# Layer norm's 1/sqrt as a power on GpSimd, first loads in halves, and a new order of the first block in a fused norm, Mish and filter kernel

## The chip, the core and the metric

One core of a Trainium2 chip runs the whole program. It has five engines, each with its own instruction stream: TensorE (PE in the profile) multiplies matrices, VectorE (DVE) and ScalarE (ACT) compute on tiles, GpSimd (POOL) does so too, and SyncE (SP) here only issues transfers. ACT can issue transfers as well. The engines meet only where one waits for what another has produced. The metric is the time of one execution on the device in microseconds; each comparison takes the median of several.

## What is computed

The input x has 2,048 rows (time) of 640 columns. Each row is normalized, and the output is x plus two branches of the normalized rows: a filter along time with a kernel built from the parameters, and a dense layer to 1,728 columns, Mish, and a dense layer back to 640.

```
xn  = (x - mean(x)) / sqrt(var(x) + 1e-5)            # per row
A   = causal_conv(xn, K) + xn * D_skip               # K from log_A, A_imag, C, dt: 128 modes
h   = xn @ w1 + b1                                    # 640 -> 1728
B   = (h * tanh(softplus(h))) @ w2                    # Mish, 1728 -> 640
out = x + A + B
```

For the parameters given here the modes hardly decay or turn, so the filter is computed as two running sums along time. The kernel tests on the chip whether the values allow this and its number formats, and holds a general path for other values, which does not run here.

## The kernel before, in words

**Numbers.** Products of float32 precision are made from float16 matmuls: every operand is split into a high part, rounded to float16, and a low part, the float16 of what is left. A product takes three matmuls: high by high, low by high, high by low. ScalarE makes the high parts (`hi_w1`, L371; `hi_w2`; `hi0`, L844), VectorE the low parts (`lo_w1`, L375; `lo_w2`, L382; `lo0`, L847).

**Tiling.** The rows are four blocks `b` of 512 (four tiles of 128 rows), the 1,728 columns are 14 groups `f`, of 128 columns but for one of 64 (f = 8), and the 640 columns are five chunks `k` of 128. Step (b, f) (`step`, L761) multiplies block b with group f of w1 into one PSUM bank (`mm1`, L545), passes it through Mish on ScalarE and VectorE (`mish_...`, L607 to L657), and three steps later multiplies the result with group f of w2 into five accumulators (`mm2`, L566). Block 0's steps also load w1 and w2 and split them. Next to this, each step has side work in lists that `place` (L676) fills: `LOADS` are transfers, `A_` and `E_` go to ScalarE, `V_` and `W_` to VectorE, earlier and later in the step. Side work is: the statistics of the next block's four tiles (steps 2 to 5), their 1/sqrt (`rstd` at step 5, L755, with `rstd_ops`, L401: thirteen small VectorE operations, a bit trick and three Newton steps, and a copy), a transpose and a round trip through DRAM that spread mean and 1/sqrt over the partitions (`spread`, L415, step 7), normalizing and splitting the next block (steps 8 to 13; `norm_t`, `hi_x` at L385, `lo_x`), the parameters of the filter (`mode_ops`, L439, cut into pieces by the list at L693), the filter itself in blocks 1 to 3, and the tests.

**The order** is written out by hand: each engine runs its instructions in the order of the program, and waits where an operand is not there yet. A tile's buffer is taken again when its last reader is done; the eight buffers of the weights (tag `w`) are such a ring.

**Block 0's beginning** is code of its own (L810 to L933). Tiles 0 and 1 fill the first 256 columns of the transposed block (slice `CA`), tiles 2 and 3 the other 256 (`CB`). The four tiles of x are loaded; VectorE computes mean and variance (`stat_ops`, L395: two halves, then an aggregation). The root is computed by both engines: ScalarE takes a square root (`sqrt0`, L814) and VectorE refines it and takes reciprocals (`rstd0`, L818), for tiles 0 and 1 together, then for 2 and 3 one by one. Tiles 0 and 2 are normalized on VectorE (`norm0`, L828), 1 and 3 on ScalarE (`norm0_a`, L831). TensorE, which has run 15 filler products (`fill`, L850), transposes a tile in five pieces (`to_t0`, L840), ScalarE takes the high parts (`hi0`) and VectorE the low parts (`lo0`), and TensorE multiplies with the first three groups of w1 piece by piece (`mm1_part`, L538, L543): first for CA, then for CB. In the order of each engine, the statistics of tile 2 precede the low part of w1(0) on VectorE, and those of tile 3 follow it. The first transfers stand at L856 to L870:

```
for i in range(2):
    sp.dma_start(X0[:, i, 0:320], xr[0, i, :, 0:320])
    a.dma_start(X0[:, i, 320:D], xr[0, i, :, 320:D])
load_w1(0)
a.dma_start(X0[:, 2], xr[0, 2])
sp.dma_start(X0[:, 3], xr[0, 3])
load_w1(1, a)
a.activation(warm, one, AF.Sqrt)
```

The last of these lines loads ScalarE's table for the square root; another one loads that of the sigmoid at L902.

## Time and profile before

| | us |
|---|---|
| median of 3 runs | 374.67 (374.29, 374.67 and 1362.29) |
| the profiled execution, its own time | 374.67 |
| its span, first to last instruction | 372.9 |
| TensorE busy | 361.2 |
| VectorE busy | 322.2 |
| ScalarE busy | 272.7 |
| GpSimd busy | 0.9 |

Times in the profile are us from the start of the span. A row of a timeline gives start, duration, engine, line of the kernel, operation, output and inputs by the program's names, shapes, how many instructions are merged, and in brackets how long the engine had been idle before and what ended that. "PEld" is the load of weights into TensorE, which overlaps its products. Matmuls overlap each other, so that a duration of one is more than its distance to the next. "xh", "xl", "w1h", "w1l" are high and low parts. Rows of GpSimd are rough in their spans.

### The profile page before, as it was taken

The page shows a single profiled execution, that of the slowest core. Times are in us where ns is not written, and L with a number is a line of the kernel's source. Part 1 is how long each engine was busy: PE and PEld are TensorE (multiplying, and loading weights), DVE is VectorE, ACT ScalarE, POOL GpSimd, SP SyncE. Part 2 cuts the span into 40 slices and gives each one's busy share as a digit, 9 for nine tenths or more (in the row PEclk, how much of TensorE's full clock was granted, in tenths as well). Part 3 has the DMA queues.
Part 4 walks back from the last instruction along what each step waited for, and adds up shares of the span by engine and source line. Part 5 has one row for each costly group of instructions (what it writes and reads, how often), then busy time and mean ns, then how long its engine had stood idle before and what let it go on. Part 6 is the DMA issues. An engine that isn't in the chain of part 4 may idle for free.

```text
span 372.9 us, 5013 instructions
## 1 busy us (share of the span) xinstructions
PE 361.2 (97%) x1737; PEld 168.8 (45%) x1737; DVE 322.2 (86%) x591; ACT 272.7 (73%) x525; POOL 0.9 (0%) x9
## 2 busy tenths in 40 slices
PE   7899999999999999999999999999999999999992
PEld 6654444444444444444444444444444444444441
DVE  4979988999997999778779999978896899999952
ACT  4799866979866858788858875598977676788540
POOL 1000000000000000000000000000000000000000
PEclk9999999999999999999999999999999999999998
DMA  7756953590002163412752252512410021300003
GB/s 261 261 159 216 307 192 127 144 352 0 2 0 73 38 198 82 153 38 70 238 167 66 60 179 83 174 39 88 127 48 32 0 78 64 113 0 2 0 7 142
DMA packets 23039, 40.81 MB, mean 109 GB/s; under 512 B 3080, under 2 KB 6432, under 8 KB 23008
## 3 DMA queue, kind: packets, MB, share of 16 engines
q1 hardware_dynamic: 22432, 39.45, 33.0%
q10 hardware_dynamic: 576, 0.98, 0.8%
q8 instruction: 15, 0.25, 0.3%
q14 instruction: 16, 0.13, 0.1%
HBM read 35.17 MB, written 5.26 MB: 108 GB/s over the span
## 4 chain that ended last, share of the span: by engine, by line
PE 73%; DVE 14%; ACT 7%; issue 2%; DMA 2%; ACTq 0%; DVEq 0%
PE h L564 35%; PE acc L591 10%; PE acc L593 10%; PE acc L592 10%; DMA x<-in_A_u_dram 2%; DVE A L640 2%; DVE A L632 1%; DVE g L518 1%; DVE g L523 1%; DVE lo L656 1%; ACT hi L646 1%; PE h L543 1%; ACT s L616 1%; PE acc L586 1%; PE acc L575 1%
## 5 line engine op out<-in xcount | busy, mean ns | idle before, releaser
L564 PE MATMUL h<-xh,w1h 128*128 128x512 f16 x265 | 92.0, 379 | 0.4 <-ACT xh L386 0.3
L593 PE MATMUL acc<-hi,w2l 128*128 128x512 f16 x235 | 89.1, 379 | 0.0
L592 PE MATMUL acc<-lo,w2h 128*128 128x512 f16 x235 | 89.1, 379 | 0.0
L591 PE MATMUL acc<-hi,w2h 128*128 128x512 f16 x235 | 89.1, 379 | 0.0
L564 PE MATMUL h<-xh,w1l 128*128 128x512 f16 x245 | 86.3, 379 | 0.0
L564 PEld LDWEIGHTS <-w1h 128*128 128x128 f16 (+1 forms) x534 | 50.5, 98 | 63.7 <-issue 4.6
L564 PE MATMUL h<-xl,w1h 128*128 128x512 f16 (+2 forms) x269 | 63.8, 377 | 0.0
L646 ACT ACTIVATE hi<-A 128x512 f16<-128x512 f32 (+1 forms) x56 | 35.0, 624 | 36.7 <-DVE A L640 36.7
L616 ACT ACTIVATE s<-h,cv 128x512 f32<-128x512 f32 x51 | 34.6, 678 | 28.3 <-PE h L564 27.1
L620 DVE SCALAR_TENSOR_TENSOR A<-h,bs,s 128x512 f32<-128x512 f32 x51 | 38.0, 745 | 12.7 <-ACT s L616 12.5
L656 DVE SCALAR_TENSOR_TENSOR lo<-A,hi 128x512 f16<-128x512 f32 x52 | 35.7, 687 | 11.7 <-ACT hi L646 11.6
L628 ACT ACTIVATE p<-p,kc 128x512 f32<-128x512 f32 (+1 forms) x56 | 40.4, 722 | 1.7
L624 ACT ACTIVATE p<-s,kc 128x512 f32<-128x512 f32 (+1 forms) x56 | 39.8, 710 | 0.1
L636 ACT ACTIVATE s<-p,kc 128x512 f32<-128x512 f32 (+1 forms) x56 | 39.8, 710 | 0.0
L632 DVE SCALAR_TENSOR_TENSOR A<-p,A 128x512 f32<-128x512 f32 (+1 forms) x56 | 38.1, 681 | 1.5 <-ACT p L628 1.5
L640 DVE SCALAR_TENSOR_TENSOR A<-s,A 128x512 f32<-128x512 f32 (+1 forms) x56 | 38.1, 681 | 0.2
L564 PEld LDWEIGHTS <-w1l 128*128 128x128 f16 x245 | 24.0, 98 | 29.3 <-issue 0.9
L591 PEld LDWEIGHTS <-w2h 128*128 128x128 f16 x235 | 23.1, 98 | 27.6
L593 PEld LDWEIGHTS <-w2l 128*128 128x128 f16 x235 | 23.0, 98 | 27.8
L592 PEld LDWEIGHTS <-w2h 128*128 128x128 f16 x235 | 23.0, 98 | 27.3
L518 DVE TENSOR_TENSOR_SCAN g<-g,car,kc 128x512 f32<-128x512 f32 x20 | 25.6, 1278 | 0.0
L523 DVE TENSOR_TENSOR_SCAN g<-g,car,g 128x512 f32<-128x512 f32 x20 | 25.4, 1270 | 0.0
(151 smaller groups left out, 357.3 us busy)
## 6 DMA issues: line engine op xcount, KB each, us to landing
res<-in_xT_dram SPq DMA_DIRECT2D x20, 256.0 KB, 5.4
out_dram<-xt SPq DMA_DIRECT2D x19, 256.0 KB, 2.7
chk<-in_w2T_dram SPq DMA_DIRECT2D x15, 288.0 KB, 3.1
w2s<-in_B_w_dram SPq DMA_DIRECT2D x13, 320.0 KB, 3.3
chk<-in_w1T_dram SPq DMA_DIRECT2D x13, 320.0 KB, 3.7
w1s<-in_w_dram SPq DMA_DIRECT2D x12, 320.0 KB, 5.0
xrow<-in_A_u_dram SPq DMA_DIRECT2D x12, 320.0 KB, 4.0
xt<-in_xT_dram SPq DMA_DIRECT2D x15, 256.0 KB, 5.8
```

Source lines behind the costliest of these rows:

```text
L564: pe.matmul(o, w, x, start=(j == 0), stop=(j == len(order) - 1))
L591: pe.matmul(ACC[k], W2H[f][:, c[k]], hi, start=False, stop=False)
L592: pe.matmul(ACC[k], W2H[f][:, c[k]], lo, start=False, stop=False)
L593: pe.matmul(ACC[k], W2L[f][:, c[k]], hi, start=False, stop=en)
L616: a.activation(s, h, AF.Sigmoid, bias=cv[:n, f:f + 1], scale=1 / SH)
L624: a.activation(p, s, AF.Arctan, bias=one[:n], scale=-1.0)
L628: a.activation(p, p, AF.Square, bias=pi4[:n], scale=2.0)
L632: v.scalar_tensor_tensor(A, p, MR, A, op0=OP.add, op1=OP.mult)
L636: a.activation(s, p, AF.Square, bias=mb[:n])
L640: v.scalar_tensor_tensor(A, s, MC, A, op0=OP.add, op1=OP.mult)
L646: a.activation(hi[:n], A, AF.Copy, scale=MA * SA / SH)
L656: v.scalar_tensor_tensor(lo, A, MA * SA / SH, hi[:n], op0=OP.mult, op1=OP.subtract)
```

## The change

- **The root.** `rstd_ops`, `sqrt0` and `rstd0` are gone. A new `rstd(var, out)` has two GpSimd instructions: add 1e-5, then raise to the power -0.5, the exponent being a constant column that takes the place of the square root's bias. In block 0 it runs for each tile by itself, right behind its statistics; in the other blocks once per block at step 5, followed by the copy of the means, on GpSimd as well.
- **First loads.** w1(0) and tiles 2 and 3 of x are loaded in halves of 64 partitions, one half on SP's queue and one on ACT's. w1(1) is loaded on SP's queue, behind tile 3. ScalarE's first table is that of the sigmoid, and there is no second load of a table in block 0's beginning.
- **The first block.** All four tiles are normalized on VectorE. The low part of w1(0) runs ahead of the statistics of tile 2. Two low parts of x (slice CA) run between the statistics of tiles 2 and 3, the others around the normalizing of tile 3. The pieces are taken in the order k = 4, 0, 1, 2, 3 (`KS`). ScalarE's high part of w1(0) stands behind tile 0's transposes in the program, ahead of the high parts of x, as before.
- **Side work.** The low parts of w2(12) and w2(13) move from step (0, 13) to steps (1, 0) and (1, 1). Of the filter's parameter operations, 13 and 15 run in steps (0, 6) and (0, 7) in place of 11 and 11, and the six of step (0, 13) are gone from there.

```
--- before.py
+++ after.py
@@ -309,9 +309,9 @@
 
 
     kc = cst.tile([P, 8], F32, name="kc")
-    for i, c in enumerate((EPS / 4, 1.0, -math.pi / 4, MB, 0.0)):
+    for i, c in enumerate((-0.5, 1.0, -math.pi / 4, MB, 0.0)):
         v.memset(kc[:, i:i + 1], c)
-    eps4, one, pi4, mb, zero = (kc[:, i:i + 1] for i in range(5))
+    half, one, pi4, mb, zero = (kc[:, i:i + 1] for i in range(5))
     warm = kc[:, 5:6]
     ident = cst.tile([P, P], F32, name="ident")
     make_identity(nc, ident)
@@ -347,10 +347,12 @@
     W1S, W2S, XT, RES, XROW, ACT, SM, NX, CHK, SK, ML = ({} for _ in range(11))
     NCHK = NF + 3 * KD
 
-    def load_w1(f, e=sp):
+    def load_w1(f, queues=(sp,)):
         W1S[f] = row.tile([P, KD, P], F32, name="w1s", tag="w", bufs=8)
-        n = FC[f]
-        e.dma_start(W1S[f][:, :, :n], w1[D * FO[f]:D * (FO[f] + n)].rearrange("(p k f) -> p k f", p=P, k=KD))
+        n, m = FC[f], P // len(queues)
+        for j, e in enumerate(queues):
+            o = D * FO[f] + j * m * KD * n
+            e.dma_start(W1S[f][j * m:(j + 1) * m, :, :n], w1[o:o + m * KD * n].rearrange("(p k f) -> p k f", p=m, k=KD))
 
     def load_w2(f):
         W2S[f] = row.tile([P, D], F32, name="w2s", tag="w", bufs=8)
@@ -398,19 +400,10 @@
         yield lambda: v.bn_stats(st[:, 1], xt[:, 320:640])
         yield lambda: v.bn_aggr(mv[:, i], st)
 
-    def rstd_ops(mv, y):
-
-        hv = tmp.tile([P, NT], F32, name="hv")
-        t = tmp.tile([P, NT], F32, name="t_rs")
-        yi = y.bitcast(I32)
-        yield lambda: v.tensor_scalar(y, mv[:, :, 1], EPS, None, op0=OP.add)
-        yield lambda: v.tensor_scalar(hv, y, 0.5, None, op0=OP.mult)
-        yield lambda: v.tensor_scalar(yi, yi, 1, None, op0=OP.logical_shift_right)
-        yield lambda: v.tensor_scalar(yi, yi, -1, 0x5f3759df, op0=OP.mult, op1=OP.add)
-        for _ in range(3):
-            yield lambda: v.tensor_tensor(t, y, y, op=OP.mult)
-            yield lambda: v.tensor_tensor(t, t, hv, op=OP.mult)
-            yield lambda: v.scalar_tensor_tensor(y, t, 1.5, y, op0=OP.subtract, op1=OP.mult, reverse0=True)
+    def rstd(var, out):
+
+        g.tensor_scalar(out, var, EPS, None, op0=OP.add)
+        g.tensor_tensor(out, out, half.to_broadcast(list(out.shape)), op=OP.pow)
 
     def spread():
 
@@ -683,14 +676,12 @@
             A_[0, f].append(lambda f=f: hi_w2(f))
             if f + 4 < NF:
                 A_[0, f].append(lambda f=f: hi_w1(f + 4))
-            if f > 0:
-                V_[0, f].append(lambda f=f: lo_w2(f - 1))
-                if f + 3 < NF:
-                    V_[0, f].append(lambda f=f: lo_w1(f + 3))
-        W_[0, LAST].append(lambda: lo_w2(LAST))
+            if f > 0 and f + 3 < NF:
+                V_[0, f].append(lambda f=f: lo_w1(f + 3))
+            V_[(0, f + 1) if f < LAST - 1 else (1, f - LAST + 1)].append(lambda f=f: lo_w2(f))
 
         LOADS[0, 4].append(lambda: SM.update(ops=mode_ops(load_par())))
-        for at, n in (((0, 6), 11), ((0, 7), 11), ((0, 13), 6), ((1, 0), 8), ((1, 1), 99)):
+        for at, n in (((0, 6), 13), ((0, 7), 15), ((1, 0), 8), ((1, 1), 99)):
             W_[at].append(lambda n=n: [o() for _, o in zip(range(n), SM["ops"])])
 
         LOADS[1, 0].append(lambda: xt_alloc(0))
@@ -702,7 +693,7 @@
                 LOADS[b, i].append(lambda b=b, i=i: load_x(b + 1, i))
                 W_[b, i + 2].append(lambda b=b, i=i: stats(b + 1, i))
             LOADS[b, 5].append(lambda b=b: load_xt(b + 1))
-            W_[b, 5].append(rstd)
+            W_[b, 5].append(rstds)
             PEX[b, 7] = spread
             for k in range(KD):
                 W_[b, 8 + k].append(lambda b=b, k=k: norm_t(b + 1, k, NX["bc"]))
@@ -752,10 +743,9 @@
         for k in range(KD):
             sp.dma_start(XT[b][:, k], xT[k * P:(k + 1) * P, b * TB:(b + 1) * TB])
 
-    def rstd():
-        for o in rstd_ops(NX["mv"], NX["st"][:, 1]):
-            o()
-        v.tensor_copy(NX["st"][:, 0], NX["mv"][:, :, 0])
+    def rstds():
+        rstd(NX["mv"][:, :, 1], NX["st"][:, 1])
+        g.tensor_copy(NX["st"][:, 0], NX["mv"][:, :, 0])
 
 
     def step(b, f):
@@ -809,21 +799,7 @@
 
     X0 = big.tile([P, NT, D], F32, name="x0", tag="bigA")
     mv0 = tmp.tile([P, NT, 2], F32, name="mv0")
-    rs0 = tmp.tile([P, 3, NT], F32, name="rs0")
-
-    def sqrt0(i, n):
-
-        a.activation(rs0[:, 0, i:i + n], mv0[:, i:i + n, 1], AF.Sqrt, bias=eps4, scale=0.25)
-
-    def rstd0(i, n):
-
-        h, r, w = (rs0[:, j, i:i + n] for j in range(3))
-        yield lambda: v.tensor_scalar(w, mv0[:, i:i + n, 1], EPS, 0.25, op0=OP.add, op1=OP.mult)
-        yield lambda: v.reciprocal(r, h)
-        for q in range(n):
-            yield lambda q=q: v.scalar_tensor_tensor(h[:, q:q + 1], w[:, q:q + 1], r[:, q:q + 1], h[:, q:q + 1],
-                                                     op0=OP.mult, op1=OP.add)
-        yield lambda: v.reciprocal(h, h)
+    rs0 = tmp.tile([P, 2, NT], F32, name="rs0")
 
     def norm0(i):
         v.tensor_scalar(X0[:, i], X0[:, i], mv0[:, i, 0:1], rs0[:, 0, i:i + 1], op0=OP.subtract, op1=OP.mult)
@@ -832,13 +808,16 @@
         v.scalar_tensor_tensor(rs0[:, 1, i:i + 1], mv0[:, i:i + 1, 0], -1.0, rs0[:, 0, i:i + 1], op0=OP.mult, op1=OP.mult)
         a.activation(X0[:, i], X0[:, i], AF.Identity, bias=rs0[:, 1, i:i + 1], scale=rs0[:, 0, i:i + 1])
 
+
+    KS = (KD - 1, *range(KD - 1))
+
     def flat0(k, c):
 
         j = k if c == CA else k + 6 if k < KD - 1 else KD
         return ACC[j // 2][:, (CA, CB)[j % 2]]
 
     def to_t0(i):
-        for k in range(KD):
+        for k in KS:
             pe.transpose(flat0(k, (CA, CB)[i // 2])[:, i % 2 * P:(i % 2 + 1) * P], X0[:, i, k * P:(k + 1) * P], ident)
 
     def hi0(k, c):
@@ -856,11 +835,12 @@
         for i in range(2):
             sp.dma_start(X0[:, i, 0:320], xr[0, i, :, 0:320])
             a.dma_start(X0[:, i, 320:D], xr[0, i, :, 320:D])
-        load_w1(0)
-        a.dma_start(X0[:, 2], xr[0, 2])
-        sp.dma_start(X0[:, 3], xr[0, 3])
-        load_w1(1, a)
-        a.activation(warm, one, AF.Sqrt)
+        load_w1(0, (sp, a))
+        for i in range(2, NT):
+            sp.dma_start(X0[:P // 2, i], xr[0, i, :P // 2])
+            a.dma_start(X0[P // 2:, i], xr[0, i, P // 2:])
+        a.activation(warm, one, AF.Sigmoid)
+        load_w1(1)
         load_w1(2)
         sp.dma_start(cv[:, 0:24], vec)
         load_w1(3)
@@ -869,60 +849,53 @@
         load_w2(1)
         load_w1(5)
         S = [list(stat_ops(mv0, X0[:, i], i)) for i in range(NT)]
-        R = {i: list(rstd0(i, n)) for i, n in ((0, 2), (2, 1), (3, 1))}
+
+        def stats0(i):
+            for o in S[i]:
+                o()
+            rstd(mv0[:, i:i + 1, 1], rs0[:, 0, i:i + 1])
+
         fill(15)
-        for o in S[0] + S[1]:
-            o()
-        sqrt0(0, 2)
-        for o in R[0]:
-            o()
-        norm0_a(1)
-        hi_w1(0)
+        stats0(0)
+        stats0(1)
         norm0(0)
         to_t0(0)
+        hi_w1(0)
+        norm0(1)
         to_t0(1)
-        for k in range(KD):
+        for k in KS:
             hi0(k, CA)
-        for o in S[2]:
-            o()
-        sqrt0(2, 1)
         lo_w1(0)
-        mm1_part(0, ("hh", "lh"), CA, start=True)
+        stats0(2)
+        mm1_part(0, ("hh",), CA, start=True, ks=KS)
+        mm1_part(0, ("lh",), CA)
         hi_w1(1)
+        lo0(KS[0], CA)
+        lo0(KS[1], CA)
         mm1_part(1, ("hh",), CA, start=True)
         hi_w1(2)
+        stats0(3)
+        norm0(2)
         mm1_part(2, ("hh",), CA, start=True)
-        for o in S[3]:
-            o()
-        sqrt0(3, 1)
-        for o in R[2]:
-            o()
-        norm0(2)
         to_t0(2)
-        a.activation(warm, one, AF.Sigmoid)
-        lo0(0, CA)
-        for o in R[3][:2]:
-            o()
-        lo0(1, CA)
-        for o in R[3][2:]:
-            o()
-        norm0_a(3)
-        for k in range(2, KD):
-            lo0(k, CA)
-        for k in range(KD):
+        lo0(KS[2], CA)
+        norm0(3)
+        lo0(KS[3], CA)
+        lo0(KS[4], CA)
+        for j, k in enumerate(KS):
+            if j == 2:
+                to_t0(3)
             for f in range(3):
-                mm1_part(f, ("hl",), CA, stop=f == 0 and k == KD - 1, ks=[k])
-            if k == 2:
-                to_t0(3)
-        for k in range(KD):
+                mm1_part(f, ("hl",), CA, stop=f == 0 and j == KD - 1, ks=[k])
+        for k in KS:
             hi0(k, CB)
         lo_w1(1)
         hi_w1(3)
-        mm1_part(0, ("hh", "lh"), CB, start=True)
-        for k in range(KD):
+        mm1_part(0, ("hh", "lh"), CB, start=True, ks=KS)
+        for k in KS:
             lo0(k, CB)
         mm1_part(1, ("hh",), CB)
-        mm1_part(0, ("hl",), CB, stop=True)
+        mm1_part(0, ("hl",), CB, stop=True, ks=KS)
         lo_w1(2)
         lo_w1(3)
         for f in (1, 2):
```

## The prediction

> **What bounds the kernel now.** I read the page first: its head, the busy times, and the chain that ended last.
>
> ```profile
> span 372.9 us, 5013 instructions
> PE 361.2 (97%) x1737; PEld 168.8 (45%) x1737; DVE 322.2 (86%) x591; ACT 272.7 (73%) x525; POOL 0.9 (0%) x9
> ```
>
> TensorE is busy 361.2 of 372.9 us and VectorE 322.2. The share alone does not say that TensorE sets the end everywhere, so the list of what TensorE waited for comes next; of its six entries this is the only one behind the first block (engine, line and what it waited for: us in total, times, longest). With it stand the stretches of 6 us at the head, around that stall, and at the end.
>
> ```profile
> PE h L564 <- ACT xh L386: 0.3, 1, 0.3
> ...
> 6.00:12.00 6.00, 3.62 (x31) 2.87 (x30) 4.51 (x17) 4.87 (x12) 0.00 (x0) 1.00 1.01 369
> 12.00:18.00 6.00, 5.65 (x49) 4.57 (x47) 5.45 (x19) 4.49 (x10) 0.00 (x0) 1.00 0.55 189
> 18.00:24.00 6.00, 6.00 (x40) 3.65 (x39) 4.11 (x7) 5.23 (x9) 0.00 (x0) 1.00 0.65 222
> ...
> 84.00:90.00 6.00, 6.00 (x29) 2.74 (x28) 5.96 (x10) 5.11 (x9) 0.00 (x0) 1.00 0.00 0
> 90.00:96.00 6.00, 5.66 (x27) 2.50 (x26) 5.97 (x10) 5.49 (x13) 0.00 (x0) 1.00 0.01 3
> ...
> 366.00:372.00 6.00, 0.00 (x0) 0.00 (x0) 0.48 (x2) 0.00 (x0) 0.00 (x0) 0.82 0.40 138
> ```
>
> A row gives the stretch, its length, then busy time and instructions of TensorE, its weight loads, VectorE, ScalarE (ACT) and GpSimd, the granted clock, and the transfers. TensorE is complete from 18 us on, but for 0.34 us at about 93 us, where the first matmuls of block 1 wait for the last high part of its input (L386); the granted clock is 1.00 throughout. The matmuls end before 366 us, and the last 7 us are the drain of the output, which the change does not touch. So only two things can shorten the run: an earlier start of the unbroken stretch, and the 0.3 us at 93. VectorE work taken away anywhere else is off the path.
>
> The unbroken stretch begins in the first block. Its rows in order of time (start, duration, engine, line, operation, and in brackets the idle time before it and what ended that):
>
> ```profile
> 1.45 5.13 PE L852 MATMUL tr<-ident 128*128 128x128 f32 x30 [1.45 <-POOL car L329]
> 3.46 0.49 DVE L397 BATCH_NORM_STATS2 st<-x 128x6 f32<-128x320 f32 x1 [2.48 <-DMA x<-in_A_u_dram]
> 4.38 0.21 DVE L399 BATCH_NORM_AGGREGATE mv<-st 128x2 f32<-128x12 f32 x1
> 4.51 0.44 DVE L397 BATCH_NORM_STATS2 st<-x 128x6 f32<-128x320 f32 x1
> 5.38 0.21 DVE L399 BATCH_NORM_AGGREGATE mv<-st 128x2 f32<-128x12 f32 x1
> 6.81 0.61 DVE L829 TENSOR_SCALAR x<-x,mv,rs 128x640 f32<-128x640 f32 x1
> 6.93 0.92 ACT L833 ACTIVATE x<-x,rs 128x640 f32<-128x640 f32 x1 [1.01 <-DVE rs L832]
> 7.92 0.74 ACT L373 ACTIVATE w1h<-w1s 128x640 f16<-128x640 f32 x1
> 8.57 1.46 ACT L845 ACTIVATE xh<-acc 128x256 f16<-128x256 f32 x5
> 8.66 0.50 DVE L397 BATCH_NORM_STATS2 st<-x 128x6 f32<-128x320 f32 x1 [1.25 <-DMA x<-in_A_u_dram]
> 9.71 0.79 DVE L377 SCALAR_TENSOR_TENSOR w1l<-w1s,w1h 128x640 f16<-128x640 f32 x1
> 10.07 1.39 ACT L373 ACTIVATE w1h<-w1s 128x640 f16<-128x640 f32 x2
> 11.54 0.71 PE L543 MATMUL h<-xh,w1h 128*128 128x256 f16 x5
> 12.11 0.61 DVE L829 TENSOR_SCALAR x<-x,mv,rs 128x640 f32<-128x640 f32 x1
> 12.63 0.42 DVE L848 SCALAR_TENSOR_TENSOR xl<-acc,xh 128x256 f16<-128x256 f32 x1
> 14.06 0.92 ACT L833 ACTIVATE x<-x,rs 128x640 f32<-128x640 f32 x1 [0.68 <-DVE rs L832]
> 15.03 0.77 PE L842 MATMUL acc<-ident,x 128*128 128x128 f32 x5
> 16.29 0.27 PE L543 MATMUL h<-xh,w1h 128*128 128x256 f16 x1
> ```
>
> Tile 2 of x landing at 8.64 us releases VectorE; it computes the statistics of tile 2, the low part of the first weights and the statistics of tile 3, and normalizes tile 2 at 12.11. Tile 3 is normalized on ScalarE only at 14.06, since VectorE has to finish its root between the low parts, and its transposes come at 15.03. **My yardstick is the row at 16.29**, the first matmul on the second half of the columns (CB): all of the rest hangs on it without a gap.
>
> **The change part by part.**
>
> *Loads.* x tiles 0 and 1 stay as they are. The first weights w1(0) and tiles 2 and 3 go in halves on the SP and ACT queues; w1(1) moves from ACT's queue to SP's, behind its half of tile 3.
>
> ```profile
> x<-in_A_u_dram ACTq DMA_DIRECT2D x1, 320.0 KB, 7.0
> x<-in_A_u_dram SPq DMA_DIRECT2D x1, 320.0 KB, 7.3
> SPq L353 <- DMA x<-in_A_u_dram: 3.2, 2, 2.1
> 3.62 0.33 SPq L353 DMA_DIRECT2D w1s<-in_w_dram  x1
> w1s<-in_w_dram SPq DMA_DIRECT2D x1, 320.0 KB, 6.8
> ```
>
> Tile 2 had 320 KB of x ahead of it on ACT's queue, 640 KB with itself. It still has 160 + 160 + 160 KB ahead of each half, 640 KB with itself. So I give it the old landing, 8.64, and no gain. Tile 3 (2.12 + 7.3 = 9.4) is needed only after 10; no gain. w1(0) is complete after 480 KB per queue in place of 640 KB. The x tiles 0 and 1 (320 KB per queue) were there by 4.51, when VectorE read tile 1 without a wait, and 640 KB were at 8.64: half way is 6.6. Its old landing is bounded by its first use at 7.92. I take 7.2, between these.
>
> Eight loads were issued without a wait and the ninth, w1(2) at 3.62, waited for an x tile: the third row says that this queue waits for earlier loads. After the change the first eight are x0, x1, w1(0) and x2 in halves, so both halves of tile 3 wait until about 3.5 to 3.9 and w1(1), w1(2) until about 4.5 to 5. On ACT's queue the wait holds back only the table load, as ACT has nothing else before 7. There is still half of the first 1,280 KB to move then, so the engines do not run dry, and the bytes ahead of w1(2) are the old 2,240 KB: it lands again at 3.62 + 6.8 = 10.4. That is a term with almost no slack (first rival).
>
> *The root.* Removed from VectorE and ScalarE: one square root, two reciprocals and their helpers per group. In its place GpSimd runs an add and a power per tile. GpSimd has run no such operation here; what it ran are these (the second computes on 128 columns), and the longest arithmetic for the same function is the sequence on VectorE in step (0, 5):
>
> ```profile
> 0.24 0.10 POOL L983 MEMSET const-float32-0.0<- 128x1 f32 x1 [0.24 <-issue]
> 1.11 0.29 POOL masks.py:199 TENSOR_SCALAR_AFFINE_SELECT ident<-ident 128x128 f32<-128x128 f32 x1
> ...
> 46.00 0.17 DVE L406 TENSOR_SCALAR st_row<-mv 128x4 f32<-128x4 f32 x1
> 48.48 0.16 DVE L758 COPY st_row<-mv 128x4 f32<-128x4 f32 x1
> ```
>
> Call G the time from finished statistics to a usable root. Below: two operations of 0.10, 0.2 us. Above: the thirteen operations from 46.00 to 48.48, 2.5 us. I take 0.7: two operations at the 0.29 of the only computing row, and 0.1 for handing over; it is nearer to the lower rows since both operate on one column.
>
> The Trainium skill (GPSIMD Engine Reference, section 2.1, Instruction dispatch) states that the first call to freshly loaded GpSimd code pays about 6 us with no instruction in the profile. The memset of 0.10 and the select of 0.29 above are first calls of two kinds, and nothing of that size stands before either. By the page the sum would come out slower, as in the third rival; by the rows it stays.
>
> *The new order of the first block, with G = 0.7.* Statistics of tile 0 end at 4.59 (4.38 + 0.21), of tile 1 at 5.59; the roots are there at 5.3 and 6.3. Both tiles are normalized on VectorE, 0.61 each, at 5.6 and 6.3, done at 6.9 (before: 6.81 to 7.85 on two engines). The filler on TensorE ends at 6.58; the ten transposes then run to about 7.6. ACT: w1(0) at 7.2, high part until 7.9, the five high parts of x (1.46) until 9.4; so the products with them end at about 9.6 and the low-weight products at 10.2. VectorE: low part of w1(0) 7.95 to 8.75, and now ahead of tile 2's statistics; these until 9.8 (1.05 from start to the next operation, 8.66 to 9.71), two low parts of x (0.35 each) until 10.5, tile 3's statistics until 11.55, tile 2 normalized until 12.15. That is 0.55 us before the old 12.72. The root of tile 3 is ready at 12.25 and one low part of x runs meanwhile; tile 3 is normalized on VectorE at 12.5 to 13.1, before: ready at 14.98. ACT has the high parts of w1(1) and w1(2) done at 11.2 (as before: 10.07 + 1.39 = 11.46, bound by their landing), TensorE their products at 11.9. Tile 2's transposes: 12.2 to 12.8; six low-x products, 0.11 each (five take 0.71, one alone 0.27), to 13.4; tile 3's transposes to 13.95; nine more products to 14.95. **The CB products start at 14.95 in place of 16.29: 1.3 us gained.** The five high parts for CB run on ACT from 14.1 to 15.6, faster than TensorE uses them (two products, 0.22, per part, the last pair at 15.8), so no new gap follows. The low parts of weights 1, 2 and 3 move up with VectorE by the same amount.
>
> How much of G is free: the first two roots may end as late as VectorE has them done for tile 2's landing, and tile 3's root has about 0.6 us to spare; with both, up to G = 1.3 nothing is lost. Beyond, the roots stand three times in a row on the path: CB = 11.05 + 3 G.
>
> *The later blocks.* The thirteen operations and their copy go to GpSimd, 2.55 us of VectorE in steps (0, 5), (1, 5) and (2, 5). They are needed by a transpose on TensorE two steps later, over 5 us after 46.00: G of either size is covered there. The gain itself lies under full TensorE, except that it leads on to the stall at 93.
>
> ```profile
> 51.57 0.11 PE tr L419
> ...
> 50.53 0.63 ACT L646 ACTIVATE hi<-A 128x512 f16<-128x512 f32 x1 [2.74 <-DVE A L640]
> 96.73 0.35 DVE L452 SCALAR_TENSOR_TENSOR junk<-par,dt 128x128 f32<-128x128 f32 x1
> ```
>
> In step (0, 6) ACT waits 2.74 us for VectorE behind that root, and in the stretches from 84 and 90 us VectorE is busy 5.96 and 5.97 of 6: the late high part at 93 comes from VectorE's backlog. Of the 2.55 us, the parameter operations moved into steps (0, 6) and (0, 7) take back two small ones (0.2 each, as at 46.00) and four of 0.35 (the row at 96.73), 1.8 in all. The rest, 0.75, is more than the 0.34 that TensorE waited: 0.3 gained. The two low parts of w2 that move from step (0, 13) into block 1 cost 0.8 each on VectorE (as the same shape at 9.71), where those four operations and they themselves have just been taken away; the products that read them come a whole step later. Zero.
>
> *Sum.* 1.3 + 0.3 = 1.6 us. The profiled execution took 374.67 us, 1.8 more than its span, and it is the median of the three shown. 374.7 - 1.6 = **373.1 us**.
>
> **The rivals.**
>
> *Weights bind in place of x* (0.17). w1(1) and w1(2) are issued over a microsecond later than now. ACT takes w1(2) at its landing and TensorE has these products ahead of tile 2's transposes in its order. If w1(2) lands at 11.6 in place of 10.4, then its high part ends at 12.4, products at 13.0 and CB starts at 16.0: 0.3 us gained, 0.3 more at 93, 374.1. For it: hardly 0.3 us of slack. Against: the same bytes ahead, 369 GB/s in that stretch.
>
> *The power is long* (0.13), the other side. G stands in series on VectorE's path: normalize waits for it and all behind waits, the statistics of tile 2 too. By CB = 11.05 + 3 G, it decides from G = 1.85, where CB is 16.6 and the 0.3 at 93 are eaten as well; at 2.5 GpSimd itself is behind (four in a row), CB = 19.25, 3.0 lost, 0.3 gained: 377.4. For it: no row of GpSimd computes anything like a power. Against: 0.10 and 0.29 for the rows there are.
>
> *First call late* (0.05). The first power has to wait for its code to be loaded, once. Such a load would be a transfer beside those of the first block, which took 7.0 and 7.3 us to land; with 7, the first root is there at 4.6 + 7 + 0.7 = 12.3, the second tile is normalized at 13.65, tile 2 at 17.85, and CB starts at 20.65: 4.4 lost, 0.3 gained, 378.8. The two first calls quoted, 0.10 and 0.29 with no gap ahead, speak against it. The Trainium skill's figure, in the section named above, would make it 377.8 by the same steps.
>
> *Change of over 2%* (0.02, half each way): nothing in the profile leads there; TensorE's 361 us stay.
>
> **How the numbers follow.** The forecast has 0.63. Its own bounds: if w1(0) lands at 6.6, its low part is done at 8.2, and if tile 2 is there by then (w1(0) with the same bytes ahead was, at 7.92), its statistics start at 8.2 in place of 8.75: 0.55 more. With 0.2 for the spread of the runs shown (374.29 and 374.67, the third far off) 372.3 is the lower end; G up to 1.3 changes nothing. The range reaches over the first rival and the long power to the bound of G: 372.3 to 377.4, leaving out the last two cases, 0.07. Two per cent, 7.5 us, is about what a measurement of this kernel can tell from no change: faster 0.01, same 0.97, slower 0.02.
>
> **What would show it.** Right: two GpSimd operations per tile, under 0.7 us together; normalize of tile 1 on VectorE by 7; no ACT normalize; tile 2 landing at 8.4 to 8.8; the first CB product at 14.7 to 15.3; no TensorE wait on L386 at 93; 50.53's wait of 2.74 gone. Wrong: statistics of tile 2 later than 9, TensorE waiting on w1h for weights 1 or 2 after 11, a gap on VectorE ahead of a normalize, or a new TensorE gap in block 1.

## The result, and the profile after

| us | before | after |
|---|---|---|
| median of 8 runs | 374.53 | 371.92 (371.22 to 372.69) |
| the profiled execution, its own time | 374.67 | 371.22 |
| its span | 372.9 | 369.4 |
| start of TensorE's unbroken stretch (first product of CB) | 16.29 | 14.59 |
| last product | 365.47 | 363.06 |

The ratio of the medians is 0.993, 95% interval 0.9912 to 0.9948: 2.6 us are gained. (One execution of the kernel before took 1362.29 us. It is among the eight; without it their median is 374.40 us, and 2.5 us are gained.) The forecast of 1.6 us had the sign right; the result lies 0.4 us below the low end of its range, and part of the gain came at the end of the program, where none was forecast. First the head of the page of the changed kernel:

```profile
span 369.4 us, 4983 instructions
PE 361.8 (98%) x1737; PEld 169.6 (46%) x1737; DVE 314.9 (85%) x536; ACT 269.3 (73%) x518; POOL 12.5 (3%) x26
```

TensorE's work is what it was, VectorE has lost 7.3 us, and GpSimd works 12.5 us. That is no gain by itself: the gain shows in what TensorE waited for. The list of its waits has one entry left of six, the one at the very start:

```profile
PE tr L831 <- POOL car L329: 1.5, 1, 1.5
```

The stretches that were shown of before, now (columns as there):

```profile
6.00:12.00 6.00, 5.94 (x44) 4.40 (x44) 5.10 (x13) 3.49 (x8) 2.46 (x6) 1.00 1.02 346
12.00:18.00 6.00, 6.00 (x53) 4.96 (x52) 5.43 (x12) 3.20 (x9) 0.30 (x1) 1.00 0.70 243
...
90.00:96.00 6.00, 6.00 (x30) 2.74 (x28) 4.35 (x7) 3.96 (x8) 0.00 (x0) 1.00 0.01 3
```

The hole of 2.38 us in the stretch from 6 is down to 0.06, those of 0.35 and 0.34 us from 12 and from 90 are closed, and from 90 us VectorE is busy for 4.35 us, where it was busy for 5.97. Now block 0's beginning, the rows that matter, in order of time:

```profile
4.47 0.21 DVE L401 BATCH_NORM_AGGREGATE mv<-st 128x2 f32<-128x12 f32 x1
4.77 0.23 POOL L405 TENSOR_SCALAR rs<-mv 128x1 f32<-128x1 f32 x1 [3.27 <-DVE mv L401]
5.09 0.58 POOL L406 TENSOR_TENSOR rs<-rs,kc 128x1 f32<-128x1 f32 x1
5.46 0.21 DVE L401 BATCH_NORM_AGGREGATE mv<-st 128x2 f32<-128x12 f32 x1
5.70 0.61 DVE L805 TENSOR_SCALAR x<-x,mv,rs 128x640 f32<-128x640 f32 x1
5.76 0.59 POOL L405 TENSOR_SCALAR rs<-mv 128x1 f32<-128x1 f32 x1
6.43 0.58 POOL L406 TENSOR_TENSOR rs<-rs,kc 128x1 f32<-128x1 f32 x1
6.51 0.74 ACT L375 ACTIVATE w1h<-w1s 128x640 f16<-128x640 f32 x1 [0.79 <-DMA w1s<-in_w_dram]
7.05 0.61 DVE L805 TENSOR_SCALAR x<-x,mv,rs 128x640 f32<-128x640 f32 x1 [0.74 <-POOL rs L406]
7.58 0.82 DVE L379 SCALAR_TENSOR_TENSOR w1l<-w1s,w1h 128x640 f16<-128x640 f32 x1
8.32 0.48 DVE L399 BATCH_NORM_STATS2 st<-x 128x6 f32<-128x320 f32 x1
9.44 1.41 ACT L375 ACTIVATE w1h<-w1s 128x640 f16<-128x640 f32 x2
11.01 0.56 DVE L805 TENSOR_SCALAR x<-x,mv,rs 128x640 f32<-128x640 f32 x1
11.18 0.47 POOL L405 TENSOR_SCALAR rs<-mv 128x1 f32<-128x1 f32 x1 [0.78 <-DVE mv L401]
11.73 0.57 POOL L406 TENSOR_TENSOR rs<-rs,kc 128x1 f32<-128x1 f32 x1
12.34 0.61 DVE L805 TENSOR_SCALAR x<-x,mv,rs 128x640 f32<-128x640 f32 x1 [0.43 <-POOL rs L406]
14.59 0.27 PE L536 MATMUL h<-xh,w1h 128*128 128x256 f16 x1
```

Three things are to be seen. Tile 2 no longer releases anything: its statistics at 8.32 follow VectorE's own work without a wait. What holds VectorE up is GpSimd's root, 0.74 us ahead of tile 1's normalize and 0.43 us ahead of tile 3's. And the first weights, ready on ScalarE at 6.51 + 0.74 = 7.25, then wait for VectorE, which comes free after 7.05 + 0.53 (a VectorE row lasts a little past the start of the next).

**Where the profiled 3.45 us came from.** Products with 512 columns follow each other every 0.215 us, though a row of one lasts 0.38; so a stall is read from starts. Before, at the border of block 1:

```profile
92.43 0.38 PE L564 MATMUL h<-xh,w1l 128*128 128x512 f16 x1
...
92.47 0.62 ACT L386 ACTIVATE xh<-xt 128x512 f16<-128x512 f32 x1
...
93.14 0.38 PE L564 MATMUL h<-xh,w1h 128*128 128x512 f16 x1 [0.34 <-ACT xh L386]
```

After, the same high part and the same product:

```profile
88.81 0.62 ACT L388 ACTIVATE xh<-xt 128x512 f16<-128x512 f32 x1
...
90.73 0.38 PE L557 MATMUL h<-xh,w1l 128*128 128x512 f16 x1
90.94 0.38 PE L557 MATMUL h<-xh,w1h 128*128 128x512 f16 x1
```

The stall was 93.14 - 92.43 - 0.215 = 0.50 us, not the 0.34 that the brackets show. The high part now is done 1.5 us ahead of its product. A second stall of this kind, at the border of block 3, had 0.21 us (products at 269.06 and 269.49); it shows as 0.05 us of idle time, and it is gone too (266.87 and 267.08). The account: 1.70 at CB (16.29 to 14.59), 0.50 more at block 1 (93.14 to 90.94), 0.21 more at block 3 (269.49 to 267.08), and 1.04 behind the last product (374.67 - 365.47 = 9.20 against 371.22 - 363.06 = 8.16). This execution is the fastest of its eight; the median gain is 0.8 us less.

### The profile page after: what moved, and what is told of

Its sections match the earlier page's. It is cut to its first block, busy times and chain, and to the rows that moved or that the text cites. A ratio compares the mean times of both kernels' runs of the same rounds, so it can differ in the third digit from the quotient of the medians.

```text
span 369.4 us, 4983 instructions
## 1 busy us (share of the span) xinstructions
PE 361.8 (98%) x1737; PEld 169.6 (46%) x1737; DVE 314.9 (85%) x536; ACT 269.3 (73%) x518; POOL 12.5 (3%) x26
## 4 chain that ended last, share of the span: by engine, by line
PE 98%; DVE 0%; issue 0%; POOL 0%; POOLq 0%
PE h L557 45%; PE acc L586 14%; PE acc L584 14%; PE acc L585 14%; PE h L536 2%; PE tr L831 2%; PE acc L578 1%; PE acc L581 1%; PE acc L568 1%; PE acc L579 1%; PE tr L536 1%; PE acc L821 1%; PE acc L572 1%; DVE xt L654 0%; PE acc L569 0%
## 5 line engine op out<-in xcount | busy, mean ns | idle before, releaser
L649 DVE SCALAR_TENSOR_TENSOR lo<-A,hi 128x512 f16<-128x512 f32 x52 | 35.7, 686 | 12.5 <-ACT hi L639 12.4
```

Source lines behind the costliest of these rows:

```text
L649: v.scalar_tensor_tensor(lo, A, MA * SA / SH, hi[:n], op0=OP.mult, op1=OP.subtract)
```

## The experiments

Theory: the head's gain, the later root and the end are separate terms; the head hangs on when VectorE can start the low part of w1(0), set by tile 1's root and by the landing of w1(0). Rivals: the new order alone makes the head's gain and the halves do nothing; or the halves alone do. The kernel before had medians of 374.87 us (11 runs) beside the first four kernels, 374.68 (13) beside the next four and 375.05 (13) beside the last four.

**The parts by themselves**

*The beginning alone*, that is loads, order and root of block 0 as after, the later blocks' root and the side work as before (against after; `rstd_ops` comes back with it, left out here):

```diff
...
-            if f > 0 and f + 3 < NF:
-                V_[0, f].append(lambda f=f: lo_w1(f + 3))
-            V_[(0, f + 1) if f < LAST - 1 else (1, f - LAST + 1)].append(lambda f=f: lo_w2(f))
+            if f > 0:
+                V_[0, f].append(lambda f=f: lo_w2(f - 1))
+                if f + 3 < NF:
+                    V_[0, f].append(lambda f=f: lo_w1(f + 3))
+        W_[0, LAST].append(lambda: lo_w2(LAST))
...
-        for at, n in (((0, 6), 13), ((0, 7), 15), ((1, 0), 8), ((1, 1), 99)):
+        for at, n in (((0, 6), 11), ((0, 7), 11), ((0, 13), 6), ((1, 0), 8), ((1, 1), 99)):
...
-        rstd(NX["mv"][:, :, 1], NX["st"][:, 1])
-        g.tensor_copy(NX["st"][:, 0], NX["mv"][:, :, 0])
+        for o in rstd_ops(NX["mv"], NX["st"][:, 1]):
+            o()
+        v.tensor_copy(NX["st"][:, 0], NX["mv"][:, :, 0])
```

> Only block 0's beginning is new (root on GpSimd, halves, new order); the later blocks' root and the side work are as before. Theory (the gain is 1.70 us at the head, 0.50 and 0.21 us at the borders of blocks by VectorE work taken away, the rest is spread between executions): CB products at 14.6 us, TensorE late again by about 0.5 us at the first matmuls of block 1 and by 0.2 at those of block 3, about 0.7 us slower than the changed kernel, 1.7 faster than before. Rival (the head carries all, its earlier start also removes the stalls): as fast as the changed kernel, 2.4 faster than before.

Measured: 372.59 us, ratio 0.9944 (0.9926 to 0.9961). CB starts at 14.84; the two stalls are back (products 0.66 and 0.40 us apart, so 0.45 and 0.18 us). What is missing against the whole change is about what these stalls hold.

*The later blocks' root alone* (against before):

```diff
+    v.memset(kc[:, 6:7], -0.5)
...
-        for o in rstd_ops(NX["mv"], NX["st"][:, 1]):
-            o()
-        v.tensor_copy(NX["st"][:, 0], NX["mv"][:, :, 0])
+        s, mv = NX["st"], NX["mv"]
+        g.tensor_scalar(s[:, 1], mv[:, :, 1], EPS, None, op0=OP.add)
+        g.tensor_tensor(s[:, 1], s[:, 1], kc[:, 6:7].to_broadcast([P, NT]), op=OP.pow)
+        g.tensor_copy(s[:, 0], mv[:, :, 0])
```

> The kernel before with the root of the later blocks alone on GpSimd. Theory (the root's 2.55 us of VectorE make the backlog): head as before, CB products at 16.3 us, both stalls gone, TensorE's last product 0.7 us earlier than before. Rival (the moved side work removes the first stall): the 0.50 us at block 1 stay, the 0.21 at block 3 go.

Measured: 373.40 us (one execution). CB at 16.32 as before; no stall at either border. The stretches:

```profile
90.00:96.00 6.00, 6.00 (x30) 2.73 (x28) 6.00 (x17) 3.99 (x10) 0.00 (x0) 1.00 0.01 3
264.00:270.00 6.00, 6.00 (x30) 2.74 (x28) 5.61 (x9) 4.25 (x9) 0.00 (x0) 1.00 0.65 218
```

VectorE is as full as ever from 90 us, and TensorE is complete: not the load of VectorE made the stall but the lateness of one high part behind it. This edit is the whole of the two stalls, 0.71 us. All timelines agree: in the six kernels with the later root on VectorE the stall at block 1 is there (0.45 to 0.52 us, and 1.09 in the next kernel), in the eight with it on GpSimd it is not.

*The moved side work alone* (against before):

```diff
-            if f > 0:
-                V_[0, f].append(lambda f=f: lo_w2(f - 1))
-                if f + 3 < NF:
-                    V_[0, f].append(lambda f=f: lo_w1(f + 3))
-        W_[0, LAST].append(lambda: lo_w2(LAST))
+            if f > 0 and f + 3 < NF:
+                V_[0, f].append(lambda f=f: lo_w1(f + 3))
+            V_[(0, f + 1) if f < LAST - 1 else (1, f - LAST + 1)].append(lambda f=f: lo_w2(f))
...
-        for at, n in (((0, 6), 11), ((0, 7), 11), ((0, 13), 6), ((1, 0), 8), ((1, 1), 99)):
+        for at, n in (((0, 6), 13), ((0, 7), 15), ((1, 0), 8), ((1, 1), 99)):
```

> The kernel before with the moved side work alone. Theory (it adds VectorE work ahead of the late high part and takes away only work behind it): the stall at block 1 grows from 0.50 us by up to 0.7, that at block 3 stays at 0.2. Rival: the stall at block 1 goes.

Measured: 374.55 us (one execution). Its waits of TensorE behind block 0's beginning:

```profile
PE h L564 <- ACT xh L386: 0.9, 1, 0.9
```

The stall at block 1 has grown: products at 91.75 and 93.05, 1.09 us in place of 0.50 (0.08 more are lost at 77). By itself the side work costs 0.67 us; it is free in the change because the root has left VectorE. (CB at 15.54, 0.75 earlier, hides it in the total: tile 2 happened to land at 7.9.)

*The loads alone* (against before; `load_w1` takes several queues, as in the change):

```diff
...
-        load_w1(0)
-        a.dma_start(X0[:, 2], xr[0, 2])
-        sp.dma_start(X0[:, 3], xr[0, 3])
-        load_w1(1, a)
+        load_w1(0, (sp, a))
+        for i in range(2, NT):
+            sp.dma_start(X0[:P // 2, i], xr[0, i, :P // 2])
+            a.dma_start(X0[P // 2:, i], xr[0, i, P // 2:])
         a.activation(warm, one, AF.Sqrt)
+        load_w1(1)
```

> The kernel before with the loads of the changed kernel alone (w1(0) and tiles 2 and 3 in halves of 64 partitions on two queues, w1(1) on SP). Theory (the halves themselves land tile 2 earlier, since both queues are worked off evenly): tile 2 lands at about 7.6 in place of 8.64, its statistics start then, CB products at about 15.3. Rival (as predicted: same bytes ahead, same landing; the new order brought the gain): landing at 8.4 to 8.7, CB products at 16.2.

Measured: 373.76 us (one execution). From its timeline:

```profile
7.83 0.49 DVE L399 BATCH_NORM_STATS2 st<-x 128x6 f32<-128x320 f32 x1 [0.26 <-DMA x<-in_A_u_dram]
...
15.48 0.27 PE L545 MATMUL h<-xh,w1h 128*128 128x256 f16 x1
```

Tile 2 is there 0.83 us earlier than in the profiled execution of before, and CB follows by 0.81. One execution does not show that the new loads did this: in the side work alone, with whole loads, tile 2 also came at 7.9 and CB at 15.54. What shows it is the landings of all 14 kernels, in the section on the prediction: with them tile 2 is there 0.9 us earlier in the mean. So the rival that gives the order everything falls.

**What sets the start of CB**

*The new order with whole loads* (against after):

```diff
-        load_w1(0, (sp, a))
-        for i in range(2, NT):
-            sp.dma_start(X0[:P // 2, i], xr[0, i, :P // 2])
-            a.dma_start(X0[P // 2:, i], xr[0, i, P // 2:])
+        load_w1(0)
+        a.dma_start(X0[:, 2], xr[0, 2])
+        sp.dma_start(X0[:, 3], xr[0, 3])
+        load_w1(1, (a,))
...
-        load_w1(1)
```

> The changed kernel with the loads of before (w1(0) whole on SP, tile 2 whole on ACT, tile 3 on SP, w1(1) on ACT). Theory (halves bring w1(0) and tile 2 earlier, and the new order needs w1(0) early, as its low part runs ahead of tile 2's statistics): w1(0) lands at 7 to 8 in place of 6.4, statistics of tile 2 start near 9.3 in place of 8.32, CB products at 15.3 to 15.8, 373.0 us. Rival (landings only scatter between executions, the halves are worth nothing): statistics of tile 2 at 8.3 to 8.7, CB at 14.6 to 14.9, 372.0 us.

Measured: 372.91 us, ratio 0.9951 (0.9932 to 0.9969), 1.0 us above the changed kernel. From its timeline:

```profile
8.21 0.74 ACT L375 ACTIVATE w1h<-w1s 128x640 f16<-128x640 f32 x1 [4.11 <-DMA w1s<-in_w_dram]
...
8.98 0.82 DVE L379 SCALAR_TENSOR_TENSOR w1l<-w1s,w1h 128x640 f16<-128x640 f32 x1 [1.42 <-ACT w1h L375]
...
16.00 0.27 PE L536 MATMUL h<-xh,w1h 128*128 128x256 f16 x1
```

Tile 1 is normalized by 7.6, but the low part of w1(0) waits 1.42 us for weights that land at 8.2. In the new order w1(0) binds where tile 2 did in the old one. In these single profiles the order alone gains 0.3 us of CB, the halves alone 0.8, both 1.7, which is more than their sum: each seems to make room that the other uses. The landings scatter by as much as these differences, so the sizes are rough.

*Other halves.* Tiles 2 and 3 cut by columns, as tiles 0 and 1 are (against after):

```diff
-            sp.dma_start(X0[:P // 2, i], xr[0, i, :P // 2])
-            a.dma_start(X0[P // 2:, i], xr[0, i, P // 2:])
+            sp.dma_start(X0[:, i, 0:320], xr[0, i, :, 0:320])
+            a.dma_start(X0[:, i, 320:D], xr[0, i, :, 320:D])
```

> The changed kernel with tiles 2 and 3 cut by columns (all 128 partitions, half a row each) in place of partitions. Theory (what counts is that both queues carry the same): tile 2 lands at 7.5 to 8.2, CB products at 14.6 to 14.9. Rival (the cut by partitions spreads it better over the transfer engines): landing near 8.6, CB after 15.0.

Measured: 371.97 us (one execution). Tile 2 is there at 8.00, where the theory has it. w1(0), which this edit leaves alone, is there only at 7.47; its low part starts at 8.24, and CB at 15.26, later than the theory had it. So the cut by partitions is not what brings tile 2 forward, and w1(0)'s landing sets CB again.

*A longer root.* Each root of block 0 runs a second power, whose result nobody reads (against after):

```diff
-            rstd(mv0[:, i:i + 1, 1], rs0[:, 0, i:i + 1])
+            y = rs0[:, 0, i:i + 1]
+            g.tensor_scalar(y, mv0[:, i:i + 1, 1], EPS, None, op0=OP.add)
+            g.tensor_tensor(kc[:, 7:8], y, half, op=OP.pow)
+            g.tensor_tensor(y, y, half, op=OP.pow)
```

> The changed kernel with one more power per root in block 0, its result unused: each root 0.6 us later. Theory (the roots of tiles 1 and 3 stand on the path): tile 1 normalized 0.6 to 0.7 later (7.7), tile 3's wait 0.6 longer, CB products at 15.9. Rival (the root is covered by VectorE work, landings set the pace): CB within 0.3 of 14.6.

Measured: 373.02 us (one execution). From its timeline:

```profile
6.21 0.61 DVE L805 TENSOR_SCALAR x<-x,mv,rs 128x640 f32<-128x640 f32 x1 [0.67 <-POOL rs L859]
...
7.90 0.61 DVE L805 TENSOR_SCALAR x<-x,mv,rs 128x640 f32<-128x640 f32 x1 [1.09 <-POOL rs L859]
8.43 0.82 DVE L379 SCALAR_TENSOR_TENSOR w1l<-w1s,w1h 128x640 f16<-128x640 f32 x1
...
13.91 0.61 DVE L805 TENSOR_SCALAR x<-x,mv,rs 128x640 f32<-128x640 f32 x1 [1.06 <-POOL rs L859]
```

CB moves from 14.59 to 16.17, 1.58 us for a power of some 0.56: 2.8 times, where the prediction's formula beyond its free part has 3. The rows show the three places: VectorE waits 0.67, 1.09 and 1.06 us for a root, where it waited 0, 0.74 and 0.43; that is 1.65 more. The root is on the path in series, though w1(0) landed early enough here (6.8).

*The add on VectorE*, only the power on GpSimd (against after):

```diff
-            rstd(mv0[:, i:i + 1, 1], rs0[:, 0, i:i + 1])
+            y = rs0[:, 0, i:i + 1]
+            v.tensor_scalar(y, mv0[:, i:i + 1, 1], EPS, None, op0=OP.add)
+            g.tensor_tensor(y, y, half, op=OP.pow)
```

> The changed kernel with the add of 1e-5 on VectorE in block 0, the power alone on GpSimd. Theory (root on the path, and GpSimd's add under a normalize takes 0.5 to 0.6 in place of 0.23): tile 1 normalized at 6.45 in place of 7.05, tile 3 at 11.8 in place of 12.34, CB products at 14.2, 371.5 us. Rival (landing of w1(1), w1(2) and tile 2 bind as soon as the root is shorter): CB at 14.5, 371.9 us.

Measured: 372.16 us, ratio 0.9927 (0.9904 to 0.995); CB at 14.92. From its timeline:

```profile
6.03 0.61 DVE L805 TENSOR_SCALAR x<-x,mv,rs 128x640 f32<-128x640 f32 x1
...
6.19 0.87 POOL L858 TENSOR_TENSOR rs<-rs,kc 128x1 f32<-128x1 f32 x1 [0.66 <-DVE rs L857]
7.10 0.61 DVE L805 TENSOR_SCALAR x<-x,mv,rs 128x640 f32<-128x640 f32 x1 [0.46 <-POOL rs L858]
```

The add of 0.15 us is put into VectorE's statistics, and the power, now under tile 0's normalize, takes 0.87 in place of 0.58: tile 1 is normalized at 7.10 as against 7.05. No gain; but the run does not settle what the add is worth, since TensorE sets CB here. Its filler products start every 0.213 us until the trace's first record of full clock and every 0.112 us behind it. That record stands at 7.42 here and at 6.41 in after; the filler's last product starts at 7.62 in place of 7.14, the transposes at 7.74 in place of 7.25, and the high parts of x on ScalarE, which wait for them, at 8.59 in place of 8.11.

The timelines together, with the start of what sets CB (old order: statistics of tile 2; new order: low part of w1(0)); those of the longer root, the spare power and the other order are left out, as these change what lies behind that start:

| kernel | order | loads | that start | CB | difference |
|---|---|---|---|---|---|
| before | old | whole | 8.66 | 16.29 | 7.63 |
| later root alone | old | whole | 8.69 | 16.32 | 7.63 |
| side work alone | old | whole | 7.92 | 15.54 | 7.62 |
| spare memsets (below) | old | whole | 8.85 | 16.48 | 7.63 |
| loads alone | old | halves | 7.83 | 15.48 | 7.65 |
| whole loads | new | whole | 8.98 | 16.00 | 7.02 |
| after | new | halves | 7.58 | 14.59 | 7.01 |
| after, again (below) | new | halves | 7.42 | 14.42 | 7.00 |
| column halves | new | halves | 8.24 | 15.26 | 7.02 |
| beginning alone | new | halves | 7.64 | 14.84 | 7.20 |
| add on VectorE | new | halves | 7.63 | 14.92 | 7.29 |

The last column is nearly constant for an order: nearly all scatter of CB is that of one start, and the new order is 0.3 to 0.6 us shorter from there. The two longer rests of the new order, 7.20 and 7.29, are those in which full clock came last, at 7.37 and 7.42. The starts scatter with the landings.

**The end, and spare work on GpSimd**

*Before, with an add and a power that nobody reads*, and *before, with eight memsets that nobody reads*, both on GpSimd ahead of block 0's statistics:

```diff
+    v.memset(kc[:, 6:7], -0.5)
...
+        g.tensor_scalar(kc[:, 7:8], one, EPS, None, op0=OP.add)
+        g.tensor_tensor(kc[:, 7:8], kc[:, 7:8], kc[:, 6:7], op=OP.pow)
```

> The kernel before with one add and one power on GpSimd at the start, on a spare column that nobody reads. In the kernels without GpSimd arithmetic the end of the program, from GpSimd's clear of its semaphores to the last row, took 0.5 us longer than in those with it, in all ten traces. Theory (it hangs on such operations having run): the end is 0.5 us shorter than before though nothing else changes. Rival (it hangs on the changed kernel's other differences): the end as before.

```diff
+        for _ in range(8):
+            g.memset(kc[:, 7:8], 0.0)
```

> The kernel before with eight memsets of a spare column on GpSimd at the start, an operation that it had used already. Theory (the arithmetic code matters): the end as before. Rival (the mere number of instructions in GpSimd's stream moves its end to another place of the fetched blocks): the end 0.5 us shorter.

Measured: 376.08 and 374.78 us (one execution each). The end first. GpSimd closes the program with two drains, which the trace records but the views leave out; from the first of them to the end of the span:

| GpSimd records in the trace | kernels | first drain to the end |
|---|---|---|
| 27 | before, side work alone, loads alone | 1.05 to 1.06 |
| 30 | spare power | 0.91 |
| 35 | spare memsets, beginning alone | 0.54 |
| 38 to 50 | all others, after among them (46) | 0.54 |

Eight memsets do what the change does, and the spare power hardly does: the theories of both runs fail, and 0.51 us of the end hang on how many instructions GpSimd has, not on what they compute. Why is not shown. (In the four kernels with 27 or 30 records, and in no other, the trace has one more transfer of instructions, of 8 KB, 0.3 us behind the end; whether that has to do with it is open.)

Of the other 0.53 us of the 1.04, the last landing of the output makes 0.32 (5.09 and 4.77 us behind the last product; 4.8 to 5.4 over all kernels, whichever the change). The last 0.22 goes with the halves. From the last landing to the first drain it is 1.27 to 1.28 us in all six kernels with whole loads and 1.03 to 1.05 in all eight with halves. In this stretch, by the trace's records, SyncE waits for the semaphores of the transfers one after the other, 0.06 to 0.08 us each. With the halves the program has 149 transfers in place of 146, and the last output lands on a semaphore three places later in that row, so that 14 such waits are left behind it and not 17.

The spare power did not cost the microsecond that its time seems to show. The row of its timeline in which VectorE goes on with tile 2:

```profile
9.55 0.49 DVE L398 BATCH_NORM_STATS2 st<-x 128x6 f32<-128x320 f32 x1 [1.91 <-DMA x<-in_A_u_dram]
```

Tile 2 landed only at 9.5 here. Its stretches from there (columns as before; the granted clock is the third from the right):

```profile
9.00:12.00 3.00, 0.84 (x8) 0.61 (x8) 2.42 (x6) 2.75 (x9) 0.00 (x0) 1.00 0.98 349
12.00:14.00 2.00, 2.00 (x13) 1.44 (x11) 1.86 (x11) 1.83 (x3) 0.00 (x0) 0.54 0.86 283
14.00:16.00 2.00, 2.00 (x13) 1.78 (x12) 1.57 (x8) 1.17 (x3) 0.00 (x0) 0.61 0.60 228
```

TensorE ran dry, 0.84 us of work from 9 to 12, and the granted clock then fell to 0.54 and 0.61: CB came at 17.92, 8.37 behind the start of tile 2's statistics in place of 7.63. A late landing is paid twice.

**Another order, and the change once more**

*Tile 3's statistics directly behind tile 2's*, low parts of x behind the normalize of tile 2 and of tile 3 (against after):

```diff
+        stats0(3)
+        norm0(2)
         lo0(KS[0], CA)
         lo0(KS[1], CA)
         mm1_part(1, ("hh",), CA, start=True)
         hi_w1(2)
-        stats0(3)
-        norm0(2)
+        to_t0(2)
         mm1_part(2, ("hh",), CA, start=True)
-        to_t0(2)
+        norm0(3)
         lo0(KS[2], CA)
-        norm0(3)
```

> The changed kernel with tile 3's statistics directly behind tile 2's, tile 2 normalized next, the first two low parts of x behind it, and TensorE's products with w1(2) behind tile 2's transposes. Theory (VectorE's chain from the low part of w1(0) to tile 3's root sets the pace): tile 2 normalized 0.6 us earlier, tile 3 0.5 earlier, no wait for its root, CB products 0.3 earlier than in the changed kernel of the same call, 0.3 us in time. Rival (tile 3's landing binds then): statistics of tile 3 wait, CB unchanged.

> The changed kernel again, for a second execution of its profile and its time beside the run before it. Theory (of its 2.6 us 0.7 are the two stalls, 0.5 the end, and the rest the head, which scatters with the landings): CB at 14.6 to 15.3, both stalls gone, 371.9 us. Rival (1.7 us at the head in every execution): CB at 14.6 within 0.1.

Measured: 372.26 us, ratio 0.9936 (0.9914 to 0.9958), for the other order, and 371.85, ratio 0.9923 (0.9898 to 0.9948), for the changed kernel itself, unedited. The other order takes VectorE's wait ahead of tile 3's normalize away, but CB is 15.39, 7.20 behind its low part of w1(0) at 8.19: it only moves the wait to TensorE, whose transposes of tile 2 wait 0.53 us for those low parts. Another 0.31 us TensorE waits for the high part of w1(1), whose load was late here. Tile 3's landing, the rival, did not bind. No version here beat the changed kernel clear of noise.

## Where the prediction held, and the steps that failed

The forecast added 1.3 us at the head and 0.3 at the border of block 1, and nothing at the end. The runs show 0.71 at the borders of blocks 1 and 3 and 0.73 at the end, so 1.2 of the 2.6 us of the medians are left for the head (1.8 of the 3.2 us by which the unedited second series beat the kernel before beside it; the head is known no better than that). The borders and the end together gave 1.1 us more than was forecast, and that is what was missing. The range had no room for it: its low end allowed 0.55 us more at the head and 0.2 for the spread, and nothing at the borders or the end.

**The end, 0 predicted, 0.73 measured, is the step that failed most.** The last 7 us are "the drain of the output, which the change does not touch": that put a term at nothing without a row that shows it. The change touches the end twice. With more instructions on GpSimd the stretch behind the first drain is 0.51 us shorter, and eight idle memsets do the same; with three transfers more, SyncE's waits behind the last landing are 0.22 us shorter.

**The later root, 0.3 predicted, 0.71 measured, is the second.** The mechanism held: the stall came from VectorE's backlog, and the root's removal ends it. The term was mis-sized, since the 0.34 us of shown idle time was taken for the stall (it is 0.50) and the second stall, 0.05 us shown and 0.21 long, was not seen at all: "TensorE is complete from 18 us on" went by busy time, in which the overlap of the rows hides it. The side work "zero" is right only beside the root's removal.

**The head, 1.3 predicted, 1.7 in the profiled pair.** The path was right: low part of w1(0) at 7.95 and CB 7.0 later was forecast, 7.58 and 7.01 came. Two sizes ahead of that start were wrong, and that they nearly cancel is luck.

- *w1(0) was given 7.2.* It landed at 6.48, and in the eight kernels with halves at 6.1 to 7.5, mean 6.8.
- *G was taken as 0.7; it is 1.0 to 1.4.* From the end of the aggregation to the normalize: 4.68 to 5.70 for tile 0, 5.67 to 7.05 for tile 1. The power alone takes 0.58, twice the row of 0.29 that stood for it, and an add that meets a normalize takes 0.47 to 0.59 in place of 0.23. "Up to G = 1.3 nothing is lost" was too generous with these landings: the first weights were ready at 7.25, and the root held VectorE until 7.58. The longer root cost 1.58 us of CB for 0.56, as the formula for the part beyond says. A gap on VectorE ahead of a normalize was one of the prediction's own signs of being wrong.

**Tile 2, "I give it the old landing, 8.64, and no gain", was wrong as well**, but moves the sum little: in the forecast its statistics start at 8.75, behind VectorE's own work. They started at 8.32 without a wait; a landing at 8.64 would have held them up by 0.3 us, an estimate from these two rows. By bytes per queue tile 2 should have landed as before. The time from issue to landing of the whole tile 2 was 7.0, 7.0, 6.2, 6.8, 7.9 and 7.2 us in the six kernels with whole loads (issue at 1.6), so 7.9 to 9.5, mean 8.7; in the eight with halves the trace has the last of it at 6.9 to 8.5, mean 7.8. The first weights in whole made ScalarE wait until 8.2 to 8.7 in four kernels; in halves it waited only until 6.1 to 7.5 in seven. These are the rows of after (issues at 1.63, 1.66 and 2.23):

```profile
w1s<-in_w_dram SPq DMA_DIRECT2D x1, 160.0 KB, 4.7
w1s<-in_w_dram ACTq DMA_DIRECT2D x1, 160.0 KB, 4.8
x<-in_A_u_dram SPq DMA_DIRECT2D x1, 160.0 KB, 5.0
```

The trace has 16 landing records of each load, and the load counts as landed with the last. Of tile 2 in before, the first is at 5.82 and the last at 8.64; in after, they are at 5.61 and 7.22 for SP's half and at 6.01 and 7.55 for ACT's. The first records hardly move, the gain is in the last. Why they lie closer together with halves was not found. The edit has another side that no run separates: with halves, tile 3 is issued at 3.5 and w1(1) at 4.6, in place of 2.1 both, so that less is on its way beside tile 2. The Trainium skill (DMA: Bandwidth & Descriptors, Issuing engines are not separate DMA queues) states that transfers issued from several engines share the same 16 and that this saves only the time of issuing. Here the halves of tile 2 are issued 0.6 us later than the whole was and still land earlier; as the later loads may be the reason, the runs leave open whether that goes against it.

What the single profile of before could not tell: its 8.66 is one sample. Over the kernels with the old order and whole loads, that start lies between 7.9 and 9.6.

**G in the later blocks "is covered": right.** The operations have four columns there:

```profile
L406 POOL TENSOR_TENSOR st_row<-st_row,kc 128x4 f32<-128x4 f32 x3 | 4.1, 1361 | 0.3
L405 POOL TENSOR_SCALAR st_row<-mv 128x4 f32<-128x4 f32 x3 | 2.6, 857 | 202.8 <-DVE mv L401 118.2 <-PE h L557 84.6
```

With the copy that is 2.6 us in the mean, as long as VectorE took, and TensorE waited for none of it.

**The rivals.** Weights binding in place of x: the first weights do bind with whole loads, but w1(1) and w1(2), which the rival named, did not; their high parts ran at 9.44 to 10.85 without a wait (in the other order ScalarE did wait 0.39 us for them). The long power: G stayed well under the 1.85 from which it decides. The first call: the first power took 0.58 and the later three 0.57 to 0.58, with nothing ahead of it, so the Trainium skill's 6 us (GPSIMD Engine Reference, 2.1 Instruction dispatch) is not in this trace.

Sum in hindsight: 0.71 at the borders, 0.73 at the end, and 1.2 at the head as what is left of 2.6 (1.0 without the execution of 1362 us). The profiled pair has 1.70 at the head; the changed kernel's landings were early ones there.

## What to carry to other kernels

Where a landing releases the first long stretch, treat its time as a spread and not as a number: try the load that is needed first in halves on both queues, together with an order in which nothing else waits behind it; here the two paid more than each alone. Do not put the end of the program at nothing: here the number of GpSimd instructions and of transfers changed it by 0.73 us. Read a stall of TensorE from the starts of its products against their usual spacing; the idle time in the brackets leaves out the overlap. And before an operation is called free on an idle engine, look for what VectorE runs at that moment.
